# First weights loaded and converted first, other due steps, and second-layer blocks of 512 and 384 tokens

## The chip, the cores and the metric

The kernel runs on one core of one Trainium2 chip. The metric is device time of the whole kernel in microseconds. Its engines are TensorE (PE in the profile, PEld for its weight loads), VectorE (DVE), ScalarE (ACT), GpSimd (POOL) and SyncE (SP), which issues the DMAs.

## The reference, cut to what matters

```python
# attention over 32 memory slots: batch 8, heads 8, sequence 576, head size 64
a = exp(phi - max over s); a = a / (sum over s + 1e-9)
k_m, v_m = a^T k, a^T v                      # [b, h, 32, 64]
attn = softmax(q k_m^T / 8)                  # over the 32 slots
x = (attn v_m) as [4608 tokens, 512]
# two layers, 512 -> 2048 -> 512 each, all float32
h = x @ w1_in;  g = where(h > 0, h, exp(min(h, 0)) - 1);  x = g @ w1_out
h = x @ w2_in;  g = h * clip(h + 3, 0, 6) / 6;            out = g @ w2_out
```

The inputs may come as float64; the kernel then gets their 64 bits as two 32-bit words and makes float32 of them on the chip (the function `convert`).

## The kernel before

A float32 product is made of three TensorE passes over rounded parts (high x high, high x low, low x high), so every operand is split into a high and a low part first.

First layer. Tokens go in 16 units of 288 (two per batch); hidden channels go in 16 chunks of 128, in four blocks q of four chunks. A step is one unit and one chunk: `first` (6 matmuls, L662 to L664), `middle` (ScalarE L671, L673, L680, VectorE L675, GpSimd L682), `second` (12 matmuls, L706). The input weights are folded with the value summary of each batch (`fold`, TensorE L616, ScalarE L622, VectorE L624), so `first` multiplies the attention weights themselves. The first four units (batches 0 and 1) are done block by block, because the weights are still being converted: all four units for block q = 0, then for q = 1, and so on, 64 steps. The other twelve units run over all 16 chunks at once.

Ahead of the steps of a batch stand `load_front`, `front` or `front_first` (exponentials of phi; for batch 0 by transposes on TensorE, copied from PSUM at L488 and L491), `summary` (keys and values summed, L515; scaled at L527, transposed at L532 and copied into kt and vt at L537 and L539), `scores` (L552) and `softmax` (L568 to L595).

Conversions (`convert`) of the first layer's weights take, per pair of chunks: ScalarE L284 and L287, VectorE L289, L291, L294 and L297, GpSimd L310 (one per chunk), VectorE L312, and for the output weights ScalarE L317 and GpSimd L321 for the high and low parts. `SINGLE = 4` makes the first two fetches (four chunks of input weights) convert chunk by chunk. The first load list is: phi of batch 0, a third of its keys and values, the two fetches of first input weights, the rest of keys and values, a half of q, two fetches of output weights, and then batch 1.

Second layer. Five blocks of twice 464 or 448 tokens, a seven-product scheme in place of eight: each block has 56 steps of its first product (`product1`, L858 to L860) and 56 of its second (`product2`, L885 to L887), 6 matmuls each, 672 in all, with one column per token pair. The weights of all seven products are read again from memory for each block. VectorE and ScalarE form the operands and combine the results.

The order of the work is not written out by hand. Every task is a generator of pieces, each with an engine, a cost in us and what it needs; tasks stand in lanes with a due step. `Schedule.pick` takes, per engine, the piece with the earliest due step that can start, and lets others fill gaps ahead of it. The due steps come from `AHEAD`: a conversion of input weights is due `w_in` steps ahead of its block, one of output weights `w_out` steps ahead of its use, and the first front, summary and scores `start` steps earlier than those of other batches. The planner runs on the host, and what it yields is the order of instructions on each engine.

Of the kernel before, what the change touches and what calls it, by code (L numbers as in the profile page):

```python
# [25 lines left out]
SC = 5  # L26
# [8 lines left out]

TILES = [((h + g) % 4, g) for h in range(4) for g in range(NG)]

BLOCKS = [464] * 4 + [448]
NU = len(BLOCKS)
STARTS = [2 * sum(BLOCKS[:u]) for u in range(NU)]  # L40
NJ = FC // 2
# [7 lines left out]

ORDER = (1, 6, 2, 7, 5, 4, 3)  # L50

READ = 12

AHEAD = dict(pe=6, front=12, summary=7, scores=3, fold=2, w_in=9, w_out=6, start=20)
LATER = 3
CONVERSIONS = 4
EXTRA = (24, 26, 28, 30)
SINGLE = 4  # L60
SLACK = 0.2

LEAST = float(np.uint32(0x38100000).view(np.float32))
# [117 lines left out]
def mixer(ctx, tc, phi_t, phi_n, kv, q_t, w1i, w1o, w2i, w2o, out):  # L181
# [83 lines left out]
    def convert(n, c, name, i, f, how, *keys):  # L265

        m = c.stop - c.start  # L270
        one, two = ((0.65, 0.75), (0.95, 1.35))[m - 1]
        place = made(name, i, f, 1)
        yield Piece("act", 0.2 + 0.43 * m, ("raw", n), *keys, *(
            place["keys"] if how == "whole" else ()),
                    slots=place["slots"] if how == "whole" else ("d",))
        raw = raws[n][:, c]
        low, high = raw[:, :, :, 0], raw[:, :, :, 1]
        highf, rest = high.bitcast(F32), low.bitcast(F32)
        if how == "whole":
            top, = make(name, i, f, m, [""])  # L280
        else:
            top = new("d", [P, m, QW], "top")
        topu = top.bitcast(U32)
        act.activation(out=top, in_=highf, func=ACTF.Abs)  # L284
        if how != "seven":
            yield Piece("act", 0.2 + 0.43 * m)
            act.activation(out=rest, in_=low, func=ACTF.Copy, scale=2.0 ** -52)  # L287
        yield Piece("dve", one)
        dve.tensor_scalar(top, top, LEAST, None, op0=ALU.max)  # L289
        yield Piece("dve", one)  # L290
        dve.tensor_scalar(topu, topu, 3, 0x3FFFFFF8, op0=ALU.logical_shift_left,  # L291
                          op1=ALU.bitwise_and)
        yield Piece("dve", two)
        dve.scalar_tensor_tensor(out=topu, in0=high, scalar=0xC0000000, in1=topu,  # L294
                                 op0=ALU.bitwise_and, op1=ALU.bitwise_or)
        yield Piece("dve", one)
        dve.tensor_scalar(high, topu, 0xFF800000, None, op0=ALU.bitwise_and)  # L297
        if how == "seven":
            yield Piece("dve", two)
            dve.scalar_tensor_tensor(out=rest, in0=low, scalar=2.0 ** -52, in1=highf,  # L300
                                     op0=ALU.mult, op1=ALU.mult)
            yield Piece("dve", two)
            dve.tensor_tensor(out=top, in0=top, in1=rest, op=ALU.add)
            drop(n, c)
            tops[name, (i * FQ + f) // 2] = top
            mark("top", name, (i * FQ + f) // 2)
            return
        for x in range(m):
            yield Piece("pool", 1.2)
            pool.tensor_tensor(out=rest[:, x], in0=rest[:, x], in1=highf[:, x], op=ALU.mult)  # L310
        yield Piece("dve", two)
        dve.tensor_tensor(out=top, in0=top, in1=rest, op=ALU.add)  # L312
        drop(n, c)
        if how == "parts":
            yield Piece("act", 0.2 + 0.43 * m, **made(name, i, f, 2))
            hi, lo = make(name, i, f, m, "hl")
            act.copy(hi, top)  # L317
        for x in range(m):
            if how == "parts":
                yield Piece("pool", 1.4)  # L320
                pool.tensor_tensor(out=lo[:, x], in0=top[:, x], in1=hi[:, x].bitcast(F32),  # L321
                                   op=ALU.subtract)
            mark(name, i, f + x)
        if how == "parts":
            give("d")
# [136 lines left out]
    def front_first(b):  # L462
# [8 lines left out]
        for g in range(NG):  # L471
# [12 lines left out]
            give("x")  # L484
            give("t")
            to = pn[:, :, g * P:(g + 1) * P]
            yield Piece("dve", 0.65, early=READ)
            dve.tensor_copy(to[:, :SC - 1], many)  # L488
            give("h")
            yield Piece("dve", 0.25, early=READ)  # L490
            dve.tensor_copy(to[:last, SC - 1], few[:last])  # L491
            give("bank")
            mark("e", b, g)
        yield Piece("dve", 0.3)
# [6 lines left out]
    def summary(b, g, whole):  # L501
# [31 lines left out]
        give("nb")  # L533
        v4 = ptr.rearrange("p (h m) -> p h m", h=4)
        kr, vr = slice(64 * g, 64 * g + 64), slice(64 - 64 * g, 128 - 64 * g)
        yield Piece("dve", 0.25, early=READ)
        dve.tensor_copy(vt[b % 2][vr], v4[vr])  # L537
        yield Piece("act", 0.25, early=READ)
        act.copy(kt[b % 2][kr], v4[kr])  # L539
        give("bank")  # L540
# [91 lines left out]

    UB = 2 * HV
    items = [(u, f, q) for q in range(NQ) for u in range(UB) for f in range(q * FQ, q * FQ + FQ)]
    items += [(u, f, None) for u in range(UB, NB) for f in range(FC)]
    n2 = len(items)
    phs, gs_, sums2 = {}, {}, {}
# [201 lines left out]
    def product1(u, j, i):  # L841
# [5 lines left out]
        keys = [("op", u, i), ("ws", u, j, PLACE[i] // 4)]  # L847
        if after:
            keys.append((after, u, j))
        yield Piece("pe", 1.375 * t / 512, *keys, slots=(kind,) if begin else ())  # L850
        if begin:
            bank2[u, j, s] = new(kind, [P, t], f"p{s}")
        ps, w, x = bank2[u, j, s], ws[u, j, PLACE[i] // 4][:, PLACE[i] % 4], ops[u, i]
# [15 lines left out]
    def product2(u, i, j):  # L869
# [5 lines left out]
        keys = [("go", u, i, j), ("ws", u, "o", i, j // 4)]  # L875
        if after and j == 0:
            keys += [(after, u, "o", d) for d in range(2)]
        yield Piece("pe", 1.375 * t / 512, *keys, slots=kinds if begin and j == 0 else ())
        if begin and j == 0:
            bank2[u, "o", s] = [new(kind, [P, t], f"q{s}{d}") for d, kind in enumerate(kinds)]  # L880
        w, (hi, lo) = ws[u, "o", i, j // 4][:, j % 4], go.pop((u, i, j))
# [160 lines left out]
    fetches = sch.lane()  # L1042
    swaps, opl, oplows, streams = sch.lane(), sch.lane(), sch.lane(), sch.lane()

    def first_use(u, f):
        if u < UB:
            return (f // FQ * UB + u) * FQ + f % FQ
        return u * FC + f

    for n in range(len(items)):  # L1050
        middles[n % len(middles)].add(middle(n), due=n)
# [7 lines left out]
    for n in range(0, len(order), 2):  # L1059
        src, name, i, f = order[n]  # L1060
        how = dict(w1i="whole", w1o="parts").get(name, "seven")
        begin = UB * FC + 5 * (n - early) if how == "seven" else (i - 1) * UB * FQ
        if n < 2 * FQ:
            pre.append(fetch(n, src, i, f))
        else:
# [2 lines left out]
        for c in [slice(0, 1), slice(1, 2)] if n < SINGLE else [slice(0, 2)]:  # L1068
            x = f + c.start
            due = begin + 14 if how == "seven" else (  # L1070
                i * UB * FQ + (x if i == 0 or how == "parts" else 0)
                + LATER * (how == "parts") - AHEAD["w_in" if how == "whole" else "w_out"])
            convs[lane % CONVERSIONS].add(
                convert(n, c, name, i, x, how, ("e", 0, 0),
                        *([("step", begin)] if begin >= 0 else [])), due=due)
            lane += 1
    for n, (name, j) in enumerate((name, j) for name in ("w2i", "w2o") for j in range(NJ)):
        sevens[n % len(sevens)].add(seven(name, j), due=UB * FC + 10 * n + 19)

    kvs = [[load_kv_whole(b, n) for n in range(3)] for b in range(2)]  # L1080
    loads.add(load_front(0), kvs[0][0], *pre[:2], *kvs[0][1:], load_q(0, 0), pre[3], pre[2],
              load_q(0, 1), load_front(1), load_q(1, 0), *kvs[1], load_q(1, 1))
    for b in range(B):
        n = (b - 1) * HV * FC
        whole = b < UB // HV
        when = [n + 2, n + 10, n + 18]
        if b == UB // HV:
            when = [2 * UB * FQ, 3 * UB * FQ, 3 * UB * FQ]
        need = first_use(b * HV, 0) - AHEAD["start"] * (b == 0)
        sides[0].add(front(b) if b else front_first(b), due=need - AHEAD["front"])  # L1090
        sides[1].add(*[summary(b, g, whole) for g in range(NG)], due=need - AHEAD["summary"])
# [8 lines left out]
            for i in range(NQ):  # L1100
                folds.add(fold(b, i, FQ), due=first_use(b * HV, i * FQ) - AHEAD["fold"])
        elif b == 0:
            for q in range(NQ):
                for j in range(UB // HV):
                    folds.add(fold(j, q, 1 if j == q == 0 else FQ),
                              due=first_use(j * HV, q * FQ) - AHEAD["fold"])

    swaps.add(swap(), due=n2 - 16)
    for u in range(NU):
# [91 lines left out]
```

## Time and profile before

| what | value |
|---|---|
| median of 3 runs | 1466.34 us (1465.06 to 2794.55) |
| the profiled execution: its own time | 1463.72 us |
| its span, first to last instruction | 1461.9 us |
| TensorE (PE) busy | 1414.6 us, 97% of the span |
| VectorE (DVE) busy | 1095.0 us, 75% |
| ScalarE (ACT) busy | 817.2 us, 56% |
| GpSimd (POOL) busy | 458.8 us, 31% |
| mean granted clock of TensorE | 0.986 |

Busy time is that of instructions on an engine; matmuls overlap, so a busy TensorE is not one at its peak. The granted clock is 1.00 at 2.4 GHz and 0.50 at 1.2 GHz. The highest of the three runs stands apart from the other two, so the median is the higher of the two that agree.

### The profile page before, as it was taken

The page shows a single profiled execution, that of the slowest core. Times are in us where ns is not written, and L with a number is a line of the kernel's source. Part 1 is how long each engine was busy: PE and PEld are TensorE (multiplying, and loading weights), DVE is VectorE, ACT ScalarE, POOL GpSimd, SP SyncE. Part 2 cuts the span into 40 slices and gives each one's busy share as a digit, 9 for nine tenths or more (in the row PEclk, how much of TensorE's full clock was granted, in tenths as well). Part 3 has the DMA queues.
Part 4 walks back from the last instruction along what each step waited for, and adds up shares of the span by engine and source line. Part 5 has one row for each costly group of instructions (what it writes and reads, how often), then busy time and mean ns, then how long its engine had stood idle before and what let it go on. Part 6 is the DMA issues. An engine that isn't in the chain of part 4 may idle for free.

```text
span 1461.9 us, 25619 instructions
## 1 busy us (share of the span) xinstructions
PE 1414.6 (97%) x9464; PEld 1283.9 (88%) x9464; DVE 1095.0 (75%) x1785; ACT 817.2 (56%) x1691; POOL 458.8 (31%) x464
## 2 busy tenths in 40 slices
PE   4698999999999999999999999999999999999999
PEld 2588898989999899999998888888888888889998
DVE  5998865677586786767357896789678867986785
ACT  4677775667667676667653454355335534553453
POOL 1678984456557565656420000000000000000000
PEclk7799999999999999999999999999999999999999
DMA  9421215336546455654336468556936783676562
GB/s 363 184 80 71 102 63 178 101 112 236 174 162 204 155 180 178 200 170 167 124 111 239 170 226 338 194 182 222 370 140 209 247 352 131 210 274 270 204 234 117
DMA packets 94221, 279.41 MB, mean 191 GB/s; under 512 B 8976, under 2 KB 50960, under 8 KB 75920
## 3 DMA queue, kind: packets, MB, share of 16 engines
q1 hardware_dynamic: 94096, 277.78, 53.5%
q8 instruction: 74, 1.21, 0.3%
q14 instruction: 51, 0.42, 0.1%
HBM read 229.51 MB, written 48.23 MB: 190 GB/s over the span
## 4 chain that ended last, share of the span: by engine, by line
PE 87%; DVE 4%; issue 3%; POOL 3%; DMA 2%; ACT 1%; SPq 0%; DVEq 0%; ACTq 0%; POOLq 0%
PE acc L706 23%; PE ph L662 5%; PE ph L663 4%; PE ph L664 4%; PE pb L859 3%; PE qb L885 3%; PE qb L886 3%; PE qb L887 3%; PE pb L858 3%; PE pb L860 3%; PE pg L859 2%; PE pa L859 2%; PE qa L885 2%; PE qa L886 2%; PE qg L885 2%
## 5 line engine op out<-in xcount | busy, mean ns | idle before, releaser
L682 POOL TENSOR_TENSOR g<-e,g 128x288 fp32r<-128x288 f32 x256 | 251.4, 988 | 234.0 <-ACT g L680 214.5
L979 ACT CAST goh<-G 128x464 fp32r<-128x464 f32 (+1 forms) x280 | 155.6, 575 | 103.1 <-PE qb L887 46.2
L675 DVE SCALAR_TENSOR_TENSOR e<-e,ph 128x288 f32<-128x288 f32 x256 | 114.4, 449 | 129.8 <-ACT e L673 113.9
L981 DVE TENSOR_TENSOR gol<-G,goh 128x464 fp32r<-128x464 f32 (+1 forms) x280 | 172.7, 636 | 34.2 <-PE qb L886 14.0
L662 PE MATMUL ph<-ahi,wf 128*128 128x288 f32 x512 | 159.3, 311 | 5.2 <-DVE e L675 4.3
L680 ACT CAST g<-e 128x288 fp32r<-128x288 f32 x256 | 109.3, 431 | 90.1 <-DVE e L675 86.0
L947 ACT ACTIVATE e<-c,three 128x464 f32<-128x464 f32 (+1 forms) x120 | 81.9, 682 | 137.6 <-DVE c L924 123.4
L671 ACT ACTIVATE e<-ph 128x288 f32<-128x288 f32 x256 | 104.8, 409 | 95.3 <-PE ph L664 82.3
L663 PE MATMUL ph<-alo,wf 128*128 128x288 f32 x512 | 152.3, 298 | 1.5 <-POOL alo L595 1.4
L664 PE MATMUL ph<-ahi,wf 128*128 128x288 f32 x512 | 152.2, 297 | 0.2 <-DVE wf L624 0.2
L662 PEld LDWEIGHTS ph<-ahi,wf 128*128 128x128 f32 x512 | 96.9, 189 | 37.5 <-issue 14.3
L673 ACT ACTIVATE e<-e 128x288 f32<-128x288 f32 x256 | 114.0, 445 | 7.5
L663 PEld LDWEIGHTS ph<-alo,wf 128*128 128x128 f32 x512 | 97.2, 190 | 2.5 <-POOL alo L595 2.5
L664 PEld LDWEIGHTS ph<-ahi,wf 128*128 128x128 f32 x512 | 97.2, 190 | 0.4 <-DVE wf L624 0.4
L706 PE MATMUL acc<-g,w1o3h 128*128 128x288 f32 x512 | 94.3, 296 | 0.0
L706 PE MATMUL acc<-g,w1o0h 128*128 128x288 f32 x512 | 91.0, 303 | 2.4 <-ACT w1o0h L317 2.4
L706 PE MATMUL acc<-g,w1o1h 128*128 128x288 f32 x512 | 90.4, 297 | 2.4 <-POOL g L682 2.4
L706 PE MATMUL acc<-g,w1o2h 128*128 128x288 f32 x512 | 90.1, 295 | 0.0
L859 PE MATMUL pb<-op,ws 128*128 128x464 f32 (+1 forms) x240 | 89.1, 371 | 0.0
L885 PE MATMUL qb<-goh,ws 128*128 128x464 f32 (+1 forms) x240 | 88.9, 370 | 0.0
L886 PE MATMUL qb<-goh,ws 128*128 128x464 f32 (+1 forms) x240 | 88.9, 370 | 0.0
L887 PE MATMUL qb<-gol,ws 128*128 128x464 f32 (+1 forms) x240 | 88.9, 370 | 0.0
(156 smaller groups left out, 3690.8 us busy)
## 6 DMA issues: line engine op xcount, KB each, us to landing
ws<-w2o SPq DMA_DIRECT2D x70, 1024.0 KB, 5.1
ws<-w2i SPq DMA_DIRECT2D x40, 1024.0 KB, 7.4
ws<-w2i SPq DMA_DIRECT2D x40, 768.0 KB, 7.9
kvc<-in_kv SPq DMA_DIRECT2D x60, 256.0 KB, 5.5
q<-in_q_t SPq DMA_DIRECT2D x32, 288.0 KB, 4.7
x2d<-st SPq DMA_DIRECT2D x32, 288.0 KB, 3.7
raw<-in_w1i SPq DMA_DIRECT2D x8, 1024.0 KB, 8.7
raw<-in_w1o SPq DMA_DIRECT2D x8, 1024.0 KB, 9.3
```

The lines of the kernel that those rows point to most:

```text
L662: pe.matmul(ps, whi, xhi, start=begin and c == 0, stop=False)
L663: pe.matmul(ps, whi, xlo, start=False, stop=False)
L664: pe.matmul(ps, wlo, xhi, start=False, stop=close and c == len(passes) - 1)
L675: dve.scalar_tensor_tensor(out=e, in0=e, scalar=-1.0, in1=ps, op0=ALU.add, op1=ALU.max)
L682: pool.tensor_tensor(out=lo, in0=e, in1=hi.bitcast(F32), op=ALU.subtract)
L706: pe.matmul(acc[d], w[:, f % FQ, d * P:(d + 1) * P], g[x], start=first, stop=last)
L859: pe.matmul(ps, whi, xlo, start=False, stop=False, **more)
L885: pe.matmul(ps, whi, hi, start=begin and j == 0, stop=False, **more)
L886: pe.matmul(ps, wlo, hi, start=False, stop=False, **more)
L887: pe.matmul(ps, whi, lo, start=False, stop=j == NJ - 1, **more)
L979: act.copy(hi, x)
L981: dve.tensor_tensor(out=lo, in0=x, in1=hi.bitcast(F32), op=ALU.subtract)
```

## The change

The first fetch of input weights goes to the head of the load list, the second right behind phi and ahead of all keys and values. `convert` no longer waits for the first exponentials (`("e", 0, 0)`). `SINGLE = 0` converts the first four chunks in two pairs, and for these (n < 4) the last addition (L312) goes from VectorE to GpSimd. The copies of the first front (L488, L491) and the copy into vt (L537, in every batch) go from VectorE to ScalarE. In `AHEAD`, `w_in` goes from 9 to 5, `w_out` from 6 to 2, `start` from 20 to 10. The blocks of the second layer become three of 512 and two of 384, and the planner's cost of their products follows another formula. `FIRST`, `where` and `block_use` state the order of the first 64 steps in a more general form.

```diff
--- before.py
+++ after.py
@@ -35,7 +35,7 @@
 
 TILES = [((h + g) % 4, g) for h in range(4) for g in range(NG)]
 
-BLOCKS = [464] * 4 + [448]
+BLOCKS = [512] * 3 + [384] * 2
 NU = len(BLOCKS)
 STARTS = [2 * sum(BLOCKS[:u]) for u in range(NU)]
 NJ = FC // 2
@@ -49,15 +49,17 @@
 
 ORDER = (1, 6, 2, 7, 5, 4, 3)
 
+FIRST = [(q, b) for q in range(NQ) for b in range(2)]
+
 READ = 12
 
 
 
-AHEAD = dict(pe=6, front=12, summary=7, scores=3, fold=2, w_in=9, w_out=6, start=20)
+AHEAD = dict(pe=6, front=12, summary=7, scores=3, fold=2, w_in=5, w_out=2, start=10)
 LATER = 3
 CONVERSIONS = 4
 EXTRA = (24, 26, 28, 30)
-SINGLE = 4
+SINGLE = 0
 SLACK = 0.2
 
 LEAST = float(np.uint32(0x38100000).view(np.float32))
@@ -308,8 +310,12 @@
         for x in range(m):
             yield Piece("pool", 1.2)
             pool.tensor_tensor(out=rest[:, x], in0=rest[:, x], in1=highf[:, x], op=ALU.mult)
-        yield Piece("dve", two)
-        dve.tensor_tensor(out=top, in0=top, in1=rest, op=ALU.add)
+        if n < 4:
+            yield Piece("pool", 0.5 + 0.7 * m)
+            pool.tensor_tensor(out=top, in0=top, in1=rest, op=ALU.add)
+        else:
+            yield Piece("dve", two)
+            dve.tensor_tensor(out=top, in0=top, in1=rest, op=ALU.add)
         drop(n, c)
         if how == "parts":
             yield Piece("act", 0.2 + 0.43 * m, **made(name, i, f, 2))
@@ -484,11 +490,11 @@
             give("x")
             give("t")
             to = pn[:, :, g * P:(g + 1) * P]
-            yield Piece("dve", 0.65, early=READ)
-            dve.tensor_copy(to[:, :SC - 1], many)
+            yield Piece("act", 0.65, early=READ)
+            act.copy(to[:, :SC - 1], many)
             give("h")
-            yield Piece("dve", 0.25, early=READ)
-            dve.tensor_copy(to[:last, SC - 1], few[:last])
+            yield Piece("act", 0.25, early=READ)
+            act.copy(to[:last, SC - 1], few[:last])
             give("bank")
             mark("e", b, g)
         yield Piece("dve", 0.3)
@@ -533,8 +539,8 @@
         give("nb")
         v4 = ptr.rearrange("p (h m) -> p h m", h=4)
         kr, vr = slice(64 * g, 64 * g + 64), slice(64 - 64 * g, 128 - 64 * g)
-        yield Piece("dve", 0.25, early=READ)
-        dve.tensor_copy(vt[b % 2][vr], v4[vr])
+        yield Piece("act", 0.25, early=READ)
+        act.copy(vt[b % 2][vr], v4[vr])
         yield Piece("act", 0.25, early=READ)
         act.copy(kt[b % 2][kr], v4[kr])
         give("bank")
@@ -632,8 +638,9 @@
 
 
 
-    UB = 2 * HV
-    items = [(u, f, q) for q in range(NQ) for u in range(UB) for f in range(q * FQ, q * FQ + FQ)]
+    UB = len({b for q, b in FIRST}) * HV
+    items = [(u, f, q) for q, b in FIRST for u in range(HV * b, HV * b + HV)
+             for f in range(q * FQ, q * FQ + FQ)]
     items += [(u, f, None) for u in range(UB, NB) for f in range(FC)]
     n2 = len(items)
     phs, gs_, sums2 = {}, {}, {}
@@ -847,7 +854,7 @@
         keys = [("op", u, i), ("ws", u, j, PLACE[i] // 4)]
         if after:
             keys.append((after, u, j))
-        yield Piece("pe", 1.375 * t / 512, *keys, slots=(kind,) if begin else ())
+        yield Piece("pe", 0.08 + t / 400, *keys, slots=(kind,) if begin else ())
         if begin:
             bank2[u, j, s] = new(kind, [P, t], f"p{s}")
         ps, w, x = bank2[u, j, s], ws[u, j, PLACE[i] // 4][:, PLACE[i] % 4], ops[u, i]
@@ -875,7 +882,7 @@
         keys = [("go", u, i, j), ("ws", u, "o", i, j // 4)]
         if after and j == 0:
             keys += [(after, u, "o", d) for d in range(2)]
-        yield Piece("pe", 1.375 * t / 512, *keys, slots=kinds if begin and j == 0 else ())
+        yield Piece("pe", 0.08 + t / 400, *keys, slots=kinds if begin and j == 0 else ())
         if begin and j == 0:
             bank2[u, "o", s] = [new(kind, [P, t], f"q{s}{d}") for d, kind in enumerate(kinds)]
         w, (hi, lo) = ws[u, "o", i, j // 4][:, j % 4], go.pop((u, i, j))
@@ -1042,10 +1049,12 @@
     fetches = sch.lane()
     swaps, opl, oplows, streams = sch.lane(), sch.lane(), sch.lane(), sch.lane()
 
+    where = {(u, f): n for n, (u, f, _) in enumerate(items)}
+
     def first_use(u, f):
-        if u < UB:
-            return (f // FQ * UB + u) * FQ + f % FQ
-        return u * FC + f
+        return where[u, f]
+
+    block_use = [min(where[u, q * FQ] for u in range(UB)) for q in range(NQ)]
 
     for n in range(len(items)):
         middles[n % len(middles)].add(middle(n), due=n)
@@ -1059,7 +1068,7 @@
     for n in range(0, len(order), 2):
         src, name, i, f = order[n]
         how = dict(w1i="whole", w1o="parts").get(name, "seven")
-        begin = UB * FC + 5 * (n - early) if how == "seven" else (i - 1) * UB * FQ
+        begin = UB * FC + 5 * (n - early) if how == "seven" else block_use[i] - 4 * FQ
         if n < 2 * FQ:
             pre.append(fetch(n, src, i, f))
         else:
@@ -1068,24 +1077,26 @@
         for c in [slice(0, 1), slice(1, 2)] if n < SINGLE else [slice(0, 2)]:
             x = f + c.start
             due = begin + 14 if how == "seven" else (
-                i * UB * FQ + (x if i == 0 or how == "parts" else 0)
+                block_use[i] + (x if i == 0 or how == "parts" else 0)
                 + LATER * (how == "parts") - AHEAD["w_in" if how == "whole" else "w_out"])
             convs[lane % CONVERSIONS].add(
-                convert(n, c, name, i, x, how, ("e", 0, 0),
+                convert(n, c, name, i, x, how,
                         *([("step", begin)] if begin >= 0 else [])), due=due)
             lane += 1
     for n, (name, j) in enumerate((name, j) for name in ("w2i", "w2o") for j in range(NJ)):
         sevens[n % len(sevens)].add(seven(name, j), due=UB * FC + 10 * n + 19)
 
-    kvs = [[load_kv_whole(b, n) for n in range(3)] for b in range(2)]
-    loads.add(load_front(0), kvs[0][0], *pre[:2], *kvs[0][1:], load_q(0, 0), pre[3], pre[2],
+    kvs = [[load_kv_whole(b, n) for n in range(3)] for b in range(UB // HV)]
+    loads.add(pre[0], load_front(0), pre[1], *kvs[0], load_q(0, 0), pre[3], pre[2],
               load_q(0, 1), load_front(1), load_q(1, 0), *kvs[1], load_q(1, 1))
+    for b in range(2, UB // HV):
+        loads.add(load_front(b), *kvs[b], load_q(b, 0), load_q(b, 1))
     for b in range(B):
         n = (b - 1) * HV * FC
         whole = b < UB // HV
         when = [n + 2, n + 10, n + 18]
         if b == UB // HV:
-            when = [2 * UB * FQ, 3 * UB * FQ, 3 * UB * FQ]
+            when = [UB * FC - 32, UB * FC - 16, UB * FC - 16]
         need = first_use(b * HV, 0) - AHEAD["start"] * (b == 0)
         sides[0].add(front(b) if b else front_first(b), due=need - AHEAD["front"])
         sides[1].add(*[summary(b, g, whole) for g in range(NG)], due=need - AHEAD["summary"])
@@ -1100,10 +1111,9 @@
             for i in range(NQ):
                 folds.add(fold(b, i, FQ), due=first_use(b * HV, i * FQ) - AHEAD["fold"])
         elif b == 0:
-            for q in range(NQ):
-                for j in range(UB // HV):
-                    folds.add(fold(j, q, 1 if j == q == 0 else FQ),
-                              due=first_use(j * HV, q * FQ) - AHEAD["fold"])
+            for q, j in FIRST:
+                folds.add(fold(j, q, 1 if j == q == 0 else FQ),
+                          due=first_use(j * HV, q * FQ) - AHEAD["fold"])
 
     swaps.add(swap(), due=n2 - 16)
     for u in range(NU):
```

## Rows read from the trace of the kernel before

**Rows 1.** Core windows: length; busy PE, PEld, DVE, ACT, POOL; clock; DMA share; GB/s.

```profile
0.00:30.00 30.00, 11.87 (x126) 6.60 (x126) 15.44 (x33) 12.40 (x21) 3.18 (x10) 0.78 0.95 357
30.00:70.00 40.00, 27.96 (x242) 20.62 (x244) 37.35 (x59) 23.20 (x44) 23.83 (x19) 0.70 0.59 232
70.00:117.00 47.00, 40.32 (x311) 34.30 (x310) 44.84 (x57) 32.85 (x74) 35.10 (x28) 0.99 0.27 94
117.00:200.00 83.00, 77.66 (x597) 72.60 (x597) 70.55 (x92) 62.35 (x133) 74.81 (x64) 0.99 0.19 66
200.00:755.00 555.00, 553.47 (x4805) 516.26 (x4804) 374.57 (x609) 373.40 (x862) 321.05 (x344) 1.00 0.48 159
755.00:1458.00 703.00, 703.00 (x3390) 633.49 (x3388) 551.21 (x939) 313.00 (x559) 0.81 (x1) 1.00 0.63 229
```

**Rows 2.** Windows of line L706 alone, the matmuls of the second product.

```profile
30.00:117.00 87.00, 34.15 (x204) 31.54 (x204) 0.85 0.42 158
```

**Rows 3.** Windows of line L662 alone, a third of the first product's matmuls.

```profile
30.00:117.00 87.00, 13.98 (x41) 8.39 (x41) 0.85 0.42 158
```

**Rows 4.** Chain of work that ended last, one piece: start us, us, what.

```profile
211.49 1.59 PE acc L706 x12
```

**Rows 5.** Timeline of the head: start us, us, engine, line, what [idle before <-releaser].

```profile
17.92 0.66 PE L515 MATMUL pkv<-kvw,pn 128*32 128x128 f32 x8 [4.48 <-DMA kvw<-in_kv]
23.47 1.15 ACT L284 ACTIVATE top<-raw 128x1024 f32<-128x1024 f32 x1
31.66 0.61 PE L662 MATMUL ph<-ahi,wf 128*128 128x288 f32 x1
...
53.73 0.93 PE L706 MATMUL acc<-g,w1o0h 128*128 128x288 f32 x4 [0.36 <-ACT w1o0h L317]
```

**Rows 6.** Groups of VectorE, 0 to 30 us: busy us, mean ns | idle before <-releaser.

```profile
L488 DVE COPY pn<-pt 128x512 f32<-128x512 f32 x2 | 1.4, 692 | 7.4 <-PE pt L483 7.4
L491 DVE COPY pn<-pt 64x128 f32<-64x128 f32 x2 | 0.5, 272 | 0.0
```

**Rows 7.** Groups of VectorE from 30 to 130 us, forms apart.

```profile
L294 DVE SCALAR_TENSOR_TENSOR w1i<-raw,w1i 128x512 uint32<-128x512 uint32 x2 | 1.4, 682 | 0.0
L312 DVE TENSOR_TENSOR w1i<-w1i,raw 128x512 f32<-128x512 f32 x2 | 1.3, 666 | 0.0
L291 DVE TENSOR_SCALAR w1i<-w1i 128x512 uint32<-128x512 uint32 x1 | 1.1, 1057 | 0.0
L289 DVE TENSOR_SCALAR w1i<-w1i 128x512 f32<-128x512 f32 x1 | 1.0, 1028 | 0.0
L297 DVE TENSOR_SCALAR raw<-w1i 128x512 uint32<-128x512 uint32 x2 | 0.8, 418 | 0.0
L537 DVE COPY vt<-ptr 64x128 f32<-64x128 f32 x2 | 0.6, 284 | 0.3 <-PE ptr L532 0.3
```

**Rows 8.** Timeline: VectorE's L291 alone, then beside a GpSimd product.

```profile
14.83 0.43 DVE L291 TENSOR_SCALAR w1i<-w1i 128x512 uint32<-128x512 uint32 x1
16.58 1.09 POOL L310 TENSOR_TENSOR raw<-raw 128x512 f32<-128x512 f32 x1 [14.87 <-DVE raw L297]
16.81 1.15 DVE L291 TENSOR_SCALAR w1i<-w1i 128x512 uint32<-128x512 uint32 x1
```

**Rows 9.** Timeline of SP: first output DMAs of two 464-token blocks in turn.

```profile
859.45 0.90 SPq L1019 DMA_DIRECT2D out_t<-c  x2
1000.38 0.90 SPq L1019 DMA_DIRECT2D out_t<-c  x2
```

**Rows 10.** Timeline of TensorE: the last block, first and last of 60 matmuls.

```profile
1446.04 0.36 PE L885 MATMUL qb<-goh,ws 128*128 128x448 f32 x1
...
1457.99 0.37 PE L887 MATMUL qg<-gol,ws 128*128 128x448 f32 x1
```

**Rows 11.** Timeline: an output-weight pair taken up, and the matmuls it releases.

```profile
48.59 1.09 DVE L289 TENSOR_SCALAR top<-top 128x1024 f32<-128x1024 f32 x1
...
62.69 0.80 PE L706 MATMUL acc<-g,w1o0h 128*128 128x288 f32 x4 [2.03 <-ACT w1o0h L317]
```

## The prediction

> **What bounds the kernel now.** I read the windows of the core first, because one share for the whole span mixes stages with different limits. From 200 us to 1458 us the reader is to see a TensorE that is busy for 553.47 of 555 us and then for 703.00 of 703 us at a granted clock of 1.00, with VectorE at 68% and 78% [rows 1]. Nothing that another engine does there shortens the span; only the length of the matmul stream counts. Before 200 us it is different: TensorE is busy for 11.87 of 30 us, 27.96 of 40, 40.32 of 47 and 77.66 of 83 us, and in the middle two stretches VectorE is the full engine, with 37.35 of 40 and 44.84 of 47 us [rows 1]. Whatever time is won before 200 us moves all that follows forward one for one.
>
> How much there is to win: between 30 and 117 us the trace has 204 matmuls of the second product and 41 at the first line of the first product, whose two sister lines have as many [rows 2, 3]. Twelve such matmuls take 1.59 us in the steady stream [rows 4], 0.1325 us each. So (204 + 3 x 41) x 0.1325 = 43 us of first-layer matmuls stand in 87 us. Some 40 us are lost to waits, small matmuls and the lower clock (0.70 granted from 30 to 70 us [rows 1], between the levels of 1.2 and 2.4 GHz). That is the ceiling of any gain.
>
> The timeline then says what the head waits for. The last key/value loads release the summary matmuls at 17.92 us; the first product begins at 31.66 us, behind the summary, the scores and a softmax; the second product begins only at 53.73 us, released by the converted output weights [rows 5]. Between 31 and 53 us VectorE works through the rest of the first input weights, the next batch and the output weights one after the other. In the first 30 us, by contrast, it is busy for 15.44 us [rows 1] and has 14.6 us free, with 7.4 us of waiting ahead of the two copies of the transposes alone [rows 6].
>
> **The change part by part.** The step order, the fold order, the step at which each conversion may begin and the loads of batch 2 come out of the new formulas as they were (each new expression gives the old value for two early batches): 0 us.
>
> Work that leaves VectorE before 30 us: the copies of the first front, 2 x (0.692 + 0.272) = 1.9 us [rows 6], and two of the copies into vt, 2 x 0.29 us. They leave a stretch in which VectorE has slack, so they are worth nothing by themselves. ScalarE takes them; it is busy for 12.40 of 30 us [rows 1], so 2.5 us more fit.
>
> Work that leaves the full stretch: of the four single conversions of the first input weights, VectorE still does after 30 us two operations of 0.682 us, two of 0.666, one of 1.057, one of 1.028 and two of 0.418 us, together 5.6 us [rows 7]. With their loads first in the queue, without the wait for the first exponentials, in pairs and with the last addition on GpSimd, all of it belongs before 30 us, where 14.6 us are free. Two copies into vt of 0.284 us for the second batch [rows 7] go to ScalarE as well. Sum: 5.6 + 0.6 = 6.2 us off a full VectorE.
>
> What can follow them: the first output weights. Half of them have landed by 23.47 us, when ScalarE takes them up [rows 5], but VectorE waits with them until its other work is through. A single L294 on 512 columns takes 0.68 us [rows 7], and a pair has four such operations on 1024 columns, so some 3.3 us of VectorE work (my estimate, two thirds of 4 x 2 x 0.68 since two kinds run at higher rates) could stand before the softmax takes the engine at about 25 us. Bounds 0 and 3.3; I take 1.7, the middle, as the softmax has the earlier due time.
>
> Additions on GpSimd: a product of 512 columns takes 1.09 us there [rows 8], so an addition of 1024 takes about 2.2 us, twice; GpSimd is busy for 3.18 of 30 us [rows 1]. Cover: GpSimd's idle time. Without it: 4.4 us later weights for the first fold, which is wanted at about 25 us. But VectorE can also lose by it: L291 on 512 columns takes 0.43 us alone and 1.15 us when a GpSimd product has begun 0.23 us before it [rows 8]. I set 0, with 0 to 4.4 us as bounds, because both additions fall before 22 us in free time.
>
> The Trainium skill has a rule that speaks against this part ("SBUF — State Buffer", section "Who interferes with whom"): VectorE and GpSimd share a port pair, and whichever comes second is blocked until the other's whole instruction ends. The rows agree: that 1.15 us operation ends 0.29 us after the GpSimd product. By that rule in full the additions would take 4.4 us from VectorE to spare it 2.7 us, and the sum below would be about 3 us instead of 7.4; by the row, that price falls due only where VectorE has work waiting.
>
> The load order: one megabyte now stands ahead of the first phi, another ahead of the first keys. Phi comes later by about 1.05 MB at the 357 GB/s of this stretch [rows 1], 2.9 us, and the front's chain with it. The keys, which release the summary at 17.92 us, had the same two weight loads ahead of their last part already, so their landing stays. Cost 0 to 2 us; I take 0.5.
>
> Other due steps: conversions rank four steps later against the work of the items, on ScalarE, VectorE and GpSimd. Total work is equal; TensorE gets its g sooner between the block boundaries and may wait at them. Bounds: a gain of 5 us (the idle 83 - 77.66 = 5.3 us of TensorE from 117 to 200 us [rows 1] gone) and the loss of the third rival below. I set 0, since both ends are real.
>
> Second layer: the token counts have the same sum (4 x 464 + 448 = 3 x 512 + 2 x 384 = 2304) and each block the same 672 matmuls. A 464-column block takes 1000.38 - 859.45 = 140.93 us [rows 9], 0.2097 us a matmul. At 448 columns 60 matmuls start from 1446.04 to 1457.99 us [rows 10], 0.2025 us each. The two differ by 0.45 ns a column, and between 288 columns (0.1325) and 448 the slope is 0.44. So 512 columns take 0.2308 to 0.2313 us and 384 0.1735 to 0.1744 us, and 672 x (3 x 0.231 + 2 x 0.174) = 699.6 us, against 672 x (4 x 0.2097 + 0.2025) = 699.7 us. Bounds -1.5 and +1.5 us; I take 0. The weights are read once a block at either size; a 384 block reads them in 117 instead of 141 us, that is 229 GB/s [rows 1] times 1.2, 275 GB/s, below the 357 GB/s of the start. VectorE's fixed part weighs more in it, but from 78% it has room. The smaller last block shortens the tail by some 0.1 us.
>
> Sum: 6.2 + 1.7 - 0.5 = 7.4 us gained. Against the profiled execution (1463.7 us) that is 1456.3; the median of the runs shown is 2.6 us above that execution, so the forecast for the median is 1466.3 - 7.4 = 1459 us. Its own range, from the bounds above, is 1451 to 1465.
>
> **The rivals.** First, the freed VectorE time is worth more: the second product starts soon after the first, denser matmuls bring the full clock earlier than 70 us, and half of the 40 us ceiling comes back. For it: VectorE is all but full for 87 us there, and its operations are stretched by GpSimd's. Against it: the same VectorE work still stands between 30 and 117 us, less some 8 us of 82. 1466 - 20 = 1446 us.
>
> Second, the change does not do what it says: nothing is gained, because the first product stays behind the keys at 17.92 us and the softmax, and what is saved turns into waiting for GpSimd (74.81 of 83 us from 117 to 200 us [rows 1]), the next full engine. For it: that share. 1463 to 1467 us.
>
> Third, slower: late conversions. The lead of an output-weight conversion over its use falls from six steps to two. A step is 18 matmuls, 2.4 us, with its fold 2.65 us. The pair that VectorE takes up at 48.59 us releases the second product at 62.69 us [rows 11], 14.1 us later; six steps (15.9 us) cover that, two (5.3 us) don't. If the three remaining blocks of input channels were each late by the difference, TensorE would wait 3 x 8.8 = 26 us; with half of it hidden by items already computed, 13 us, less the 7.4 us gained: 1472 us. It decides from where VectorE or GpSimd has no gaps in which a conversion can start early; with 70.55 of 83 us busy on VectorE [rows 1] there still are some, which speaks against it.
>
> **How the numbers follow.** Forecast 0.55, first rival 0.16, second 0.16, third 0.13. The range takes in most of the first rival, all of the second, and cuts the third: 1444 to 1468 us. A measurement of this kernel tells 2%, 29 us, from no change: faster than 1437 us would need three quarters of the ceiling (0.03), slower than 1495 us the full price of the third rival and more (0.02); same 0.95.
>
> **What would show it.** In the profile after: L284 on the first input weights in two pairs, both before 15 us; their last addition on GpSimd; no work on them on VectorE after 25 us; the first product still at 31 to 33 us; the second product at about 45 us instead of 53.73; the first layer ending some 7 us earlier; 672 x 0.231 us a block in the second layer. I am wrong if the first product moves by more than 3 us, if TensorE waits for w1o at a boundary, or if a 512 or 384 block shows idle TensorE.

## The result and the profile after

The changed kernel takes 1449.82 us (median of 4 runs, 1448.16 to 1450.1) against 1465.94 us before: ratio 0.989, 95% interval 0.987 to 0.9909. One run of before at 2794.55 us is left out of that ratio as disturbed. The forecast was 1459 us with a range of 1444 to 1468: the sign was right, the gain of 16 us is more than twice the 7.4 us forecast. The profiled executions differ by 14.0 us in span (1461.9 and 1447.9).

The windows of the core, for the stretches of [rows 1] (length; busy PE, PEld, DVE, ACT, POOL; clock; DMA share; GB/s), of the kernel after:

```profile
0.00:30.00 30.00, 11.56 (x158) 6.21 (x158) 19.62 (x30) 15.74 (x29) 10.58 (x15) 0.87 0.96 367
30.00:70.00 40.00, 30.18 (x252) 21.72 (x253) 35.29 (x52) 26.63 (x52) 23.58 (x20) 0.71 0.64 251
70.00:117.00 47.00, 41.28 (x303) 37.12 (x302) 40.64 (x50) 33.31 (x75) 34.82 (x30) 0.96 0.20 72
117.00:200.00 83.00, 78.09 (x589) 72.06 (x590) 70.16 (x92) 60.43 (x128) 78.39 (x66) 0.98 0.18 62
...
755.00:1443.00 688.00, 688.00 (x3357) 609.97 (x3356) 545.03 (x937) 311.19 (x557) 0.00 (x0) 1.00 0.64 232
```

VectorE does 35.29 + 40.64 = 75.9 us between 30 and 117 us, where it did 82.2 [rows 1]: 6.3 us less, close to the 6.2 that were costed. In the first 30 us it does 4.2 us more. GpSimd is up from 3.18 to 10.58 us there.

The timeline of the head after, to be held against [rows 5] (start us, us, engine, line, what), shows the points that the prediction named:

```profile
5.79 1.12 ACT L286 ACTIVATE w1i<-raw 128x1024 f32<-128x1024 f32 x1 [3.77 <-DMA raw<-in_w1i]
10.12 1.16 ACT L286 ACTIVATE w1i<-raw 128x1024 f32<-128x1024 f32 x1
13.42 2.72 POOL L315 TENSOR_TENSOR w1i<-w1i,raw 128x1024 f32<-128x1024 f32 x1
13.93 2.77 DVE L293 TENSOR_SCALAR w1i<-w1i 128x1024 uint32<-128x1024 uint32 x1
17.44 0.26 ACT L543 COPY vt<-ptr 64x128 f32<-64x128 f32 x1 [3.46 <-PE ptr L538]
19.54 0.26 ACT L543 COPY vt<-ptr 64x128 f32<-64x128 f32 x1 [1.56 <-PE ptr L538]
31.48 0.69 DVE L291 TENSOR_SCALAR top<-top 128x1024 f32<-128x1024 f32 x1
31.96 0.59 PE L669 MATMUL ph<-ahi,wf 128*128 128x288 f32 x1
40.12 1.03 DVE L293 TENSOR_SCALAR top<-top 128x1024 uint32<-128x1024 uint32 x1
54.33 1.33 PE L713 MATMUL acc<-g,w1o0h 128*128 128x288 f32 x4
```

(L284, L291, L312, L537, L662 and L706 of before are L286, L293, L318, L543, L669 and L713 here, L315 is the addition on GpSimd.) The first product starts where it did, at 31.96 against 31.66 us. The second product starts at 54.33 us against 53.73, not at the forecast 45: between the first and the second VectorE operation of an output-weight pair lie 8.6 us, in which VectorE worked on the next batch and the next softmax.

The second layer holds the larger part of the gain. Output DMAs of two 512-token blocks and of two 384-token blocks in turn, of the timeline of SP after, answer to [rows 9]:

```profile
863.33 0.90 SPq L1026 DMA_DIRECT2D out_t<-c  x2
1015.65 0.90 SPq L1026 DMA_DIRECT2D out_t<-c  x2
...
1294.71 1.59 SPq L1026 DMA_DIRECT2D out_t<-c  x2
1410.83 0.86 SPq L1026 DMA_DIRECT2D out_t<-c  x2
```

A 512 block takes 152.32 us, 0.2267 us a matmul; the forecast had 0.2308 to 0.2313. A 384 block takes 116.1 us. TensorE's own timeline after has three steps of 0.1733 us between these two (forecast 0.1735 to 0.1744):

```profile
1443.22 0.33 PE L894 MATMUL qg<-gol,ws 128*128 128x384 f32 x1
...
1443.74 0.34 PE L894 MATMUL qg<-gol,ws 128*128 128x384 f32 x1
```

So 672 x (3 x 0.2267 + 2 x 0.1733) = 689.9 us stand in place of 699.7, 9.8 us of the 14.0. The last first-layer matmul starts at 756.52 us where it started at 760.64 before: 4.1 us come from the head. The two rows, of before and of after:

```profile
760.64 0.29 PE L706 MATMUL acc<-g,w1o3h 128*128 128x288 f32 x1
...
756.52 0.29 PE L713 MATMUL acc<-g,w1o3h 128*128 128x288 f32 x1
```

One trace of each is not exact to a microsecond: the kernel with the sizes alone has the old head too, and its first layer ends at 762.46 us; the kernel with the head alone has the new one, and ends it at 757.27 us.

### The profile page after: what moved, and what is told of

It reads as the page before. It is cut to its first block, busy times and chain, and to the rows that moved or that the text cites. A ratio compares the mean times of both kernels' runs of the same rounds, so it can differ in the third digit from the quotient of the medians.

```text
span 1447.9 us, 25617 instructions
## 1 busy us (share of the span) xinstructions
PE 1404.5 (97%) x9464; PEld 1264.6 (87%) x9464; DVE 1081.3 (75%) x1753; ACT 822.7 (57%) x1707; POOL 464.6 (32%) x466
## 4 chain that ended last, share of the span: by engine, by line
PE 85%; DMA 1%; DVE 1%; issue 0%; ACT 0%; SPq 0%; DVEq 0%; ACTq 0%
PE acc L713 22%; PE ph L669 4%; PE ph L671 4%; PE ph L670 4%; PE qb L894 3%; PE pb L865 3%; PE pb L867 3%; PE pb L866 3%; PE qb L892 3%; PE qb L893 3%; PE pa L865 2%; PE qg L894 2%; PE qa L894 2%; PE pg L865 2%; PE pa L867 2%; PE pa L866 2%
## 5 line engine op out<-in xcount | busy, mean ns | idle before, releaser
L986 ACT CAST goh<-G 128x512 fp32r<-128x512 f32 (+1 forms) x280 | 155.7, 576 | 97.0 <-PE qb L894 38.7
L682 DVE SCALAR_TENSOR_TENSOR e<-e,ph 128x288 f32<-128x288 f32 x256 | 114.4, 449 | 128.0 <-ACT e L680 109.2
L988 DVE TENSOR_TENSOR gol<-G,goh 128x512 fp32r<-128x512 f32 (+1 forms) x280 | 171.7, 635 | 25.0 <-PE qb L893 11.1
L669 PE MATMUL ph<-ahi,wf 128*128 128x288 f32 x512 | 158.1, 309 | 2.0 <-DVE e L682 2.0
L954 ACT ACTIVATE e<-c,three 128x512 f32<-128x512 f32 (+1 forms) x120 | 81.9, 682 | 134.4 <-DVE c L931 114.8
L669 PEld LDWEIGHTS ph<-ahi,wf 128*128 128x128 f32 x512 | 97.0, 190 | 30.0 <-issue 16.4
L713 PE MATMUL acc<-g,w1o0h 128*128 128x288 f32 x512 | 92.5, 304 | 3.7 <-ACT w1o0h L323 3.5
L713 PE MATMUL acc<-g,w1o3h 128*128 128x288 f32 x512 | 94.7, 296 | 0.0
L713 PE MATMUL acc<-g,w1o1h 128*128 128x288 f32 x512 | 91.2, 298 | 2.4 <-ACT w1o1h L323 2.4
L713 PE MATMUL acc<-g,w1o2h 128*128 128x288 f32 x512 | 90.0, 295 | 0.0
L867 PE MATMUL pb<-op,ws 128*128 128x512 f32 (+1 forms) x240 | 88.1, 367 | 0.0
L866 PE MATMUL pb<-op,ws 128*128 128x512 f32 (+1 forms) x240 | 88.1, 367 | 0.0
L892 PE MATMUL qb<-goh,ws 128*128 128x512 f32 (+1 forms) x240 | 88.1, 367 | 0.0
L893 PE MATMUL qb<-goh,ws 128*128 128x512 f32 (+1 forms) x240 | 88.1, 367 | 0.0
```

The lines of the kernel that those rows point to most:

```text
L669: pe.matmul(ps, whi, xhi, start=begin and c == 0, stop=False)
L682: dve.scalar_tensor_tensor(out=e, in0=e, scalar=-1.0, in1=ps, op0=ALU.add, op1=ALU.max)
L713: pe.matmul(acc[d], w[:, f % FQ, d * P:(d + 1) * P], g[x], start=first, stop=last)
L866: pe.matmul(ps, whi, xlo, start=False, stop=False, **more)
L867: pe.matmul(ps, wlo, xhi, start=False, stop=k == 1, **more)
L892: pe.matmul(ps, whi, hi, start=begin and j == 0, stop=False, **more)
```

## The experiments

Each run had the kernel before beside it on the same chip; its median there is given, as it differs by a few us from one set of runs to another.

**The sizes alone**, in the kernel before:

```diff
-BLOCKS = [464] * 4 + [448]
+BLOCKS = [512] * 3 + [384] * 2
```

> The kernel before with the block sizes alone (three of 512, two of 384). Theory one, the sizes carry most of the gain (the trace after has 0.2267 us a matmul at 512 columns and 0.1733 at 384, and 672 x (3 x 0.2267 + 2 x 0.1733) = 689.9 us against 699.7): 1465.9 - 10 = 1456 us. Theory two, as the prediction had it, sizes are neutral and the head gives all 16 us: 1465 to 1467 us.

1455.34 us against 1464.37; ratio 0.9943 (0.9926 to 0.9959). Theory one: 9.0 us are the sizes'.

**The head alone**, the kernel after with the old blocks:

```diff
-BLOCKS = [512] * 3 + [384] * 2
+BLOCKS = [464] * 4 + [448]
```

> The kernel after with the old blocks (four of 464, one of 448). Theory one: only the head's gain stays, 4 to 6 us, 1460 to 1462 us. Theory two: all 16 us stay, 1450 us. If head and sizes are independent, this run and the one with the sizes alone add up to the whole change.

1460.09 us against the same 1464.37; ratio 0.997 (0.9961 to 0.9979), 4.3 us. The two parts add up to 13.3 us, near the 14.0 us of the two traces and at the lower end of the interval of the whole (13 to 19 us). So they add up within the noise; a joint effect of some 3 us is not excluded.

**Old due steps** in the kernel after:

```diff
-AHEAD = dict(..., w_in=5, w_out=2, start=10)
+AHEAD = dict(..., w_in=9, w_out=6, start=20)
```

> The kernel after with the old due steps (9, 6, 20 in place of 5, 2, 10). If the later due steps held the output weights back (the second product begins at 54.33 us after the change, 53.73 before), it begins some 8 to 10 us earlier here and the time falls to 1444 to 1448 us. If, the other way, early conversions take VectorE from the items' own work, the time rises by 3 to 6 us, 1453 to 1456 us. The prediction's 0 would be 1450 us.

1452.67 us; ratio 0.9933 (0.9913 to 0.9952) against 0.989 for the whole change, with intervals that only just stay apart. In this kernel's timeline the output weights do come sooner, and it does not help:

```profile
50.77 1.33 PE L713 MATMUL acc<-g,w1o0h 128*128 128x288 f32 x4
...
759.54 0.29 PE L713 MATMUL acc<-g,w1o3h 128*128 128x288 f32 x1
```

The second product starts 3.6 us earlier and the first layer ends 3.0 us later than in the kernel after. In these two traces the earlier second product goes with a later end of the first layer.

**New due steps and sizes, nothing else**, in the kernel before:

```diff
-BLOCKS = [464] * 4 + [448]
+BLOCKS = [512] * 3 + [384] * 2
...
-AHEAD = dict(..., w_in=9, w_out=6, start=20)
+AHEAD = dict(..., w_in=5, w_out=2, start=10)
```

> The kernel before with the new block sizes and the new due steps, without the early loads and conversions. Against the sizes alone (1456 us by theory one): if the due steps are worth nothing by themselves, 1456 us; if the head's gain is theirs, 1450 to 1452 us; if they only cost, 1458 to 1462 us.

1457.57 us, ratio 0.9956 (0.9941 to 0.9971), on the same chip as the sizes alone (0.9926 to 0.9959): no gain by themselves. Whether they cost 2 us can't be told.

**Periods by size.** Three runs of the kernel after with other blocks of the same sum, one execution each:

```diff
-BLOCKS = [512] * 3 + [384] * 2
+BLOCKS = [512, 464, 448, 480, 400]
+BLOCKS = [512, 496, 416, 432, 448]
+BLOCKS = [512, 352, 320, 256, 416, 448]
```

> The kernel after with blocks of 512, 464, 448, 480 and 400 (same sum of 2304), so that one run has the matmul period of five sizes. Theory one, sizes that are multiples of 128 pay N + 32 cycles of 2.4 GHz and others 6 to 8 more: 480 takes (480 + 39) / 2.4 = 0.2163 us, 400 takes 0.1825 us. Theory two, only the sizes 448 and 464 are off and the rest lies on N + 32: 480 takes 0.2133 us, 400 takes 0.1800 us.

> The kernel after with blocks of 512, 496, 416, 432 and 448. Theory one: 0.2230, 0.1892, 0.1958 us at 496, 416 and 432 columns. Theory two: 0.2200, 0.1867, 0.1933 us. 448 and 512 repeat the periods of the traces, 0.2027 and 0.2267 us.

> The kernel after with six blocks, of 512, 352, 320, 256, 416 and 448. Theory one: 256 takes (256 + 32) / 2.4 = 0.1200 us, 320 takes 0.1492, 352 takes 0.1625. Theory two: 0.1200, 0.1467, 0.1600 us. The weights of a 256 block are read in 672 x 0.120 = 81 us, so its TensorE may wait for them; the period is read between the waits. The time is about 32 cycles x 672 = 9 us longer than with five blocks, 1459 us or more.

They took 1457.43, 1458.12 and 1477.3 us (before beside them: 1463.02). The third lies 18 us above the least that was expected: six blocks cost 12 us more than five by the periods below, and in its trace the 256 block takes 93 us from its first matmul to that of the next block, in place of 81, with TensorE waiting 9.1 us in that stretch for weights read from memory, as the expectation had feared. TensorE's timeline of the first of the three runs has 49 matmuls of 480 columns from the first of these rows to the second, 10.48 / 48 = 0.218 us each:

```profile
1199.64 0.38 PE L865 MATMUL pa<-op,ws 128*128 128x480 f32 x1
...
1210.12 0.38 PE L865 MATMUL pb<-op,ws 128*128 128x480 f32 x1
```

The table has the mean distance of the starts of neighbouring matmuls of one size, over 650 to 690 of them in each run (1360 to 2730 where several blocks of a kernel have the size), and what it leaves above one column per cycle of 2.4 GHz:

| columns | period, us | cycles above N |
|---|---|---|
| 256 | 0.1199 | 31.8 |
| 320 | 0.1466 | 31.8 |
| 352 | 0.1606 | 33.4 |
| 384 | 0.1734 | 32.1 |
| 400 | 0.1806 | 33.4 |
| 416 | 0.1886 | 36.7 |
| 432 | 0.1957 | 37.8 |
| 448 | 0.2027 | 38.4 |
| 464 | 0.2097 | 39.4 |
| 480 | 0.2176 | 42.1 |
| 496 | 0.2233 | 40.0 |
| 512 | 0.2267 | 32.1 |

Neither theory holds as it stood. 480 and 496 are off, against the second; 320 is not a multiple of 128 and pays 31.8, against the first. Up to 400 columns a matmul costs some 32 cycles above its columns, from 416 to 496 columns up to 42, and at 512 again 32. Sizes that occur in two kernels agree to 0.2 cycles. The two products of a block, whose operands lie in different buffers, show the same period at 464 columns (0.2097 at 800 us and at 1000 us of the trace before). That speaks against the place of an operand as the cause but does not test it; what the extra is was not found.

**Copies back on VectorE**, in the kernel after:

```diff
-            act.copy(to[:, :SC - 1], many)
+            dve.tensor_copy(to[:, :SC - 1], many)
...
-            act.copy(to[:last, SC - 1], few[:last])
+            dve.tensor_copy(to[:last, SC - 1], few[:last])
...
-        act.copy(vt[b % 2][vr], v4[vr])
+        dve.tensor_copy(vt[b % 2][vr], v4[vr])
```

> The kernel after with the copies of the first front and of vt back on VectorE. The prediction priced those before 30 us at nothing and two of 0.28 us behind it at 0.6 us: 1450 to 1451 us. If every copy on VectorE delays the first summary, 3 us of VectorE work come back and the time is 1452 to 1453 us.

1458.59 us against 1463.39; ratio 0.9966 (0.9954 to 0.9978). On the same chip the kernel of the next experiment, which has the copies on ScalarE (and the addition of the first four chunks on VectorE), takes 1449.95, 8.6 us less; by the ratios (0.9966 against 0.989) the kernel after itself is 11 us faster. The dearest expectation was 3 us. The timeline of this kernel tells a part of it:

```profile
19.10 2.70 POOL L315 TENSOR_TENSOR w1i<-w1i,raw 128x1024 f32<-128x1024 f32 x1
19.60 0.35 DVE L533 TENSOR_SCALAR kvn<-pkv,rs 128x128 f32<-128x128 f32 x1
19.87 3.02 DVE L296 SCALAR_TENSOR_TENSOR w1i<-raw,w1i 128x1024 uint32<-128x1024 uint32 x1
20.10 0.45 PE L538 MATMUL ptr<-ident,kvn 128*128 128x128 f32 x1 [0.63 <-DVE kvn L533]
22.81 0.27 DVE L543 COPY vt<-ptr 64x128 f32<-64x128 f32 x1
23.11 0.26 ACT L545 COPY kt<-ptr 64x128 f32<-64x128 f32 x1 [4.38 <-DVE vt L543]
...
36.99 0.59 PE L669 MATMUL ph<-ahi,wf 128*128 128x288 f32 x1
```

The copy into vt is wanted at 20.5 us and stands behind L296, which GpSimd's addition has stretched to 3.02 us; kt waits for vt, the scores for kt, the softmax for the scores, and the first product starts at 36.99 in place of 31.96 us. The wait behind L296 is 2.3 us of these 5.0; the copy into vt of the first half comes 0.7 us later already, and the rest is lost between the scores and the end of the softmax. The Trainium skill ("SBUF — State Buffer", section "Who interferes with whom") calls the ports that VectorE shares with GpSimd an exclusive lock and has a VectorE instruction with two inputs in SBUF, as L296 is, contend with a GpSimd instruction that reads SBUF. This row agrees: L296 ends 1.09 us, about its own free length (1.2 us), after L315 ends at 21.80.

The first layer of this kernel ends at 766.05 us, 9.5 us after that of the kernel after, so the late first product is about half of the loss. The other half lies further on. From 30 to 200 us the waits of TensorE with the largest sum in this kernel are for VectorE's L682, a step's own operation (in the kernel after they sum to 2.0 us):

```profile
PE ph L669 <- DVE e L682: 5.1, 4, 2.0
```

The edit also puts the fourteen later copies into vt back on VectorE. Whether these or the changed order of the work make the second half was not tested.

**The addition back on VectorE**, in the kernel after:

```diff
-        if n < 4:
+        if n < 0:
             yield Piece("pool", 0.5 + 0.7 * m)
```

> The kernel after with the last addition of the first four chunks back on VectorE (two of 1.2 us in place of two of 2.4 to 2.7 us on GpSimd, beside which the trace after shows VectorE's L293 at 2.77 us and L580 at 2.32 us). If GpSimd's idle time covers it, as the prediction had it, the time stays or rises by up to 2 us: 1450 to 1452 us. If the port rule decides, VectorE loses more to the additions than it is spared, and the time falls by 1 to 3 us: 1447 to 1449 us.

1449.95 us; ratio 0.9911 (0.9898 to 0.9925) against 0.989 (0.987 to 0.9909) for the whole change: no difference clear of the noise. The first product starts earlier, at 29.47 us, the second later, at 56.54, and the first layer ends at 756.64 (756.52 in the kernel after). What GpSimd's part of the change is worth is too small for these runs to tell.

**The old load list and the wait for the first exponentials**, in the kernel after:

```diff
-                convert(n, c, name, i, x, how,
+                convert(n, c, name, i, x, how, ("e", 0, 0),
...
-    loads.add(pre[0], load_front(0), pre[1], *kvs[0], load_q(0, 0), pre[3], pre[2],
+    loads.add(load_front(0), kvs[0][0], *pre[:2], *kvs[0][1:], load_q(0, 0), pre[3], pre[2],
```

> The kernel after with the old load list and the wait for the first exponentials, all else new. If the early loads make the head's gain, it is lost: 1454 to 1456 us. If pairs, copies and due steps make it, 1450 to 1452 us.

1459.64 us; ratio 0.9971 (0.996 to 0.9983), 9.7 us above the kernel with the addition on VectorE. The first product starts at 35.23, the second at 62.39 us. The first layer ends at 763.76 us. The early loads and conversions (the list and the wait were not taken apart) carry the head's gain, and so do the copies: taking away either costs about 9 us, and what is left (ratios 0.9966 and 0.9971) is no better than the sizes alone (0.9943). With the new due steps, that is: the new due steps and sizes by themselves have 0.9956.

**One product of each later conversion on VectorE**, in the kernel after:

```diff
+            late = n >= 8 and x == 1
-            yield Piece("pool", 1.2)
-            pool.tensor_tensor(out=rest[:, x], in0=rest[:, x], in1=highf[:, x], op=ALU.mult)
+            yield Piece("dve" if late else "pool", 0.75 if late else 1.2)
+            (dve if late else pool).tensor_tensor(out=rest[:, x], in0=rest[:, x],
+                                                  in1=highf[:, x], op=ALU.mult)
```

> The kernel after with one of the two products of each later conversion (L312, second chunk, blocks 1 to 3) on VectorE, 0.7 us, in place of GpSimd, 1.1 to 1.3 us. VectorE has 76 us of work between 30 and 117 us in the trace after, GpSimd 78.39 of 83 us from 117 to 200 us. If GpSimd has become the engine that limits the head, 12 x 1.2 us off it give 2 to 5 us: 1445 to 1448 us. If VectorE still limits it, as the prediction had it, 12 x 0.7 us more on it cost 3 to 6 us: 1453 to 1456 us.

1453.63 us; ratio 0.9934 (0.9922 to 0.9947), 3.7 us above the kernel with the addition on VectorE. In its windows a good part of GpSimd's load from 117 to 200 us is gone, and the kernel is slower:

```profile
117.00:200.00 83.00, 78.80 (x577) 74.02 (x578) 69.86 (x94) 55.65 (x119) 63.82 (x54) 0.93 0.17 59
```

63.82 us in place of 78.39 on GpSimd, and the first layer ends 4.5 us later. But the run did not only take load off GpSimd: its trace has the twelve products on VectorE at 13.0 us, 1.08 us each, not at the 0.7 us that were expected.

```profile
L313 DVE TENSOR_TENSOR raw<-raw 128x512 f32<-128x512 f32 x12 | 13.0, 1081 | 0.0
```

So moving this work is a loss; whether GpSimd, busy 94% of that stretch, limits the kernel after is not shown by it.

**Conversions later still**, in the kernel after:

```diff
-AHEAD = dict(..., w_in=5, w_out=2, start=10)
+AHEAD = dict(..., w_in=3, w_out=0, start=10)
```

> The kernel after with conversions due two steps later again (w_in 3, w_out 0). Going from 9 and 6 to 5 and 2 was worth 2.9 us. If the lateness itself pays (items before conversions on a full VectorE), another 1 to 2 us: 1448 to 1449 us. If the third rival of the prediction sets in, TensorE waits at the boundaries for w1o (a new wait of the L713 matmuls on L323 or L327) and the time rises by 3 us or more: 1453 us or above.

1452.65 us against 1464.59; ratio 0.9915 (0.9902 to 0.9929), 2.8 us above the changed kernel's median, with overlapping intervals. The waits of TensorE from 30 to 200 us (us in total, times, longest) show the third rival beginning, at w1o2 too:

```profile
PE acc L713 <- ACT w1o0h L323: 5.7, 2, 4.7
PE acc L713 <- ACT w1o2h L323: 3.8, 1, 3.8
```

The kernel after has these two at the boundaries of blocks 1 and 2:

```profile
PE acc L713 <- ACT w1o1h L323: 2.4, 1, 2.4
PE acc L713 <- POOL w1o2l L327: 1.2, 1, 1.2
```

No run is clearly faster than the changed kernel.

## Why the prediction was wrong in size

**Second layer.** This is the step that failed: "So 512 columns take 0.2308 to 0.2313 us and 384 0.1735 to 0.1744 us", and with it "Bounds -1.5 and +1.5 us; I take 0". The term was drawn as a straight line through 288, 448 and 464 columns. The periods don't lie on one: 448 and 464 pay 38 and 39 cycles above their columns, 512 and 384 pay 32. Measured, the term is 9.0 us (the sizes alone) to 9.8 us (by the two traces). With 9 us in its place the sum would have been 16.4 us; the change gave 16.1. That this agrees so well is partly luck, since the head's 7.4 us were too many. The forecast's own range, 1451 to 1465 us, was missed; 1449.8 lies only in the part that was added for the first rival, which did not occur. The expectation that neither size would show idle TensorE was right: 688 of 688 us are busy from 755 to 1443 us.

**Head.** Forecast 7.4 us, measured 4.3 (head alone) and 4.1 (end of the first layer): right in sign, 3 us too large.

- 6.2 us off a full VectorE: the work did go (6.3 us less from 30 to 117 us), and the head gained two thirds of that. That the one makes the other is not shown: the kernels with the old copies and with the old loads have still less on VectorE there (33.86 + 39.08 = 72.9 and 31.82 + 40.90 = 72.7 us) and end the first layer 9.5 and 7.2 us later than the kernel after. VectorE's busy time in the stretch was the wrong measure; what these two lose first is the start of the first product (36.99 and 35.23 us).
- 1.7 us for output weights before the softmax, "the second product at about 45 us": it did not happen. In the trace after VectorE takes up the weights at 31.48 us, behind the softmax, and then works on the next batch. (Two thirds of 4 x 2 x 0.68 are 3.6, not 3.3; the four operations on the first input-weight pair do take 3.3 us in the trace after.) The run with old due steps has the second product at 50.77 us and is slower, so the point that I watched did not decide the time.
- Copies "worth nothing by themselves" since VectorE has slack before 30 us: wrong by some 9 us in the kernel after (all copies into vt included). Slack was counted in the kernel before; the early conversions go into that slack, and a copy of 0.27 us in the chain to the first product then waits behind operations of up to 3.02 us. On ScalarE the chain is free of them. With the new due steps, neither early loads nor copies pay without the other.
- Addition on GpSimd at 0: not refuted (1449.95 against 1449.82 us), though L293 took 2.77 us beside it.
- Load order, 0 to 2 us: in the profile the first phi is taken up at 6.56 in place of 3.66 us, the 2.9 us that were worked out, but the last keys release the summary at 15.48 in place of 17.92 us, and the first product comes 0.3 us later. What the order costs by itself was not measured; with the conversions that it makes early it is a gain.
- Due steps at 0: about 3 us of gain with the early loads by the medians (1452.67 with the old ones) and by the end of the first layer, 6 us by the ratios; none without the early loads. Near the upper bound of 5 us or inside it.

**Rivals.** The first (a gain of 20 us in the head) did not occur. The second named GpSimd as the next full engine; its share rose to 78.39 of 83 us, and whether it limits anything stays open, since the run that took 14.6 us off it put 13.0 us on VectorE. The third is real two steps further on, at w_out 0, with TensorE waiting 3.8 us for one block. At w_out 2 TensorE does wait for w1o at two boundaries, which the prediction named as a sign against it: 2.4 us (L323, block 1) and 1.2 us (L327, block 2).

## What to carry to other kernels

Measure the matmul period at the sizes in question before cutting blocks: a line through the sizes at hand missed 10 cycles in 544 at 512 columns, and over the 2016 matmuls of that size this was 9 us, more than all the work on the head gave. When work is moved into an engine's idle time, look for the short operations of the critical chain on that same engine: they now queue behind it. A test that takes load off a suspected engine must also price the engine that gets it.

## What the runs showed of the hardware

The period of these fp32r matmuls, each with its own weight load, is not linear in the columns: 31.8 to 33.4 cycles of 2.4 GHz above N from 256 to 400 columns, 36.7 to 42.1 from 416 to 496, 32.1 at 512, at a granted clock of 0.99 to 1.00, read between neighbouring matmuls without a wait. Why stays open. VectorE's operations on 1024 columns grew from 0.68 to 2.77 us (L293, kernel after) and from 1.2 to 3.02 us (L296, copies back on VectorE) beside a GpSimd addition of 2.7 us.
